# 16-bit pairs with power-of-two scales in the feed-forward products of a state-attention and hard-swish network

## The chip, the cores and the metric

The kernel runs on one core of a Trainium2 chip. The metric is the device time of one execution in microseconds; less is better. The engines are named as the profile names them: PE (TensorE, the matrix engine; PEld is its weight load), DVE (VectorE), ACT (ScalarE), POOL (GpSimd) and SP (SyncE, which here only issues transfers).

## The reference

Eight batches of `x` (8 heads, 512 tokens, 64 wide) are attended against 32 states per head, in both directions, and all 4352 result rows pass through a feed-forward network with 2048 hidden features:

```python
scores = scale * np.matmul(x, state.transpose(0, 1, 3, 2))
...
xread = np.matmul(a, state)                # 512 token rows of a batch
scores2 = scale * np.matmul(state, x.transpose(0, 1, 3, 2))
...
sread = np.matmul(a2, x)                   # 32 state rows of a batch
x = concatenate([xread, sread])            # rows of 512 = 8 heads x 64
h = x @ w_in                               # 512 x 2048
g = h * np.clip(h + 3.0, 0.0, 6.0) / 6.0
out = (g @ w_out).astype(np.float32)       # 2048 x 512
```

(The last lines are shortened; shapes are in the comments.) Everything is 32-bit at the inputs and at the output.

## The kernel before

**Products of pairs.** A number is kept as a pair: a rounded high part `hi` and the rest `lo`, both in the reduced 32-bit format `fp32r`. `split` (L329) makes a pair with two instructions, a copy on ACT that rounds and a subtraction on DVE. `product` (L1064) multiplies two pairs with three matmuls of 128x128 by 128x512: hi.hi, hi.lo and lo.hi.

**Steps.** The work is cut into steps n = 16b + i: batch b (0 to 7) and hidden block i (0 to 15, 128 features each). Step group b = 8 holds the state rows of all batches. In `first` (L1082) six matmuls make one block of h, transposed: the stationary operand is `wp` (the product of the batch's states with `w_in`, so that h comes straight from the attention weights), the moving one is `aT` (the attention weights). ACT and DVE then form `g` (L1127, L1129) and split it (L331, L332). In `second` (L1134), two steps later (`LAG`), twelve matmuls (4 blocks of 128 tokens, three each) add `g` times `w_out` into the banks acc0 to acc3; the stationary operand is `g`, the moving one is `w_out_hi` or `w_out_lo`. After block 15 ACT and DVE empty the four banks with the factor 1/6 (L1171, L1174). Matmuls of both kinds are recorded at L1071. For b = 8, `states_halves` splits curves that are already there, and `second` has two token blocks instead of four.

**Around the steps.** `attention` (L938) computes scores and softmax of a batch ahead of its steps. `wp` is made in `wprime` (L654, matmuls at L541) for b < 4; for b from 4 on eight products of `joined` (L585, matmuls at L608) make it for four batches together, write it to memory (`far_wp`), and `wprime_loaded` (L632) reads it back. `w_in_terms` (L1243) and `states_first` (L1263) do the first product of the state rows in a form with fewer multiplications.

**What sets the order.** All instructions are added to a `Plan` with an engine, a cost, a rank, and what they read and write. `Plan.order` (L121) first follows a list of numbers (`OPENING`) and then takes, engine by engine, what can start soonest, the smaller rank first. Pools have numbered slots, which the plan gives out. Each engine runs its list in order; the waits between engines follow from the data.

```python
for l, r in ((ah, bh), (ah, bl), (al, bh)):
    nc.tensor.matmul(ps, l, r, start=start and k == 0, stop=stop and k == n - 1)
```

Of the kernel before, what the change touches and what calls it, by code (L numbers as in the profile page):

```python
# [34 lines left out]

PLAIN = 1
STATES = [110, 111, 118, 0.5, 1.0]
EARLY = 5
BY_TWO = (0, 0)
TERMS = [76, 4, 3.0]  # L40
JOINED = 4
JOINED_AT = [33, 41, 42, 49, 57, 59, 60, 70]
# [3 lines left out]
LOADED = [-6, -6.5]  # L46
STAGED = [('wp', 'ot'), ('wp', 'ot'), ('ot', 'wp'), ('ot', 'aT'), ('ot', 'wp'), ('wp', 'aT'), ('aT', 'wp'), ('ot', 'ot')]
PREP = [4, -4]
SUMS = -3
CURVE = 2  # L50
# [34 lines left out]
class Plan:  # L85
# [14 lines left out]
    def add(self, engine, cost, rank, do, reads=(), writes=(), after=(), size=0):  # L100
        n = len(self.ops)
        deps = set(after)
# [13 lines left out]

    def slot_of(self, key):

        return key[:2] if key[0] in self.slots else None

    def order(self):  # L121
        opening = [int(n) for n in OPENING.split()]
# [20 lines left out]
        row, self.start, self.took = [], [0.0] * n_ops, [0.0] * n_ops  # L143
        while len(row) < n_ops:
            best = None
            told = opening[len(row)] if len(row) < len(opening) else None
            for e, numbers in open_ops.items():
                if told is not None:
                    numbers = {told} & numbers
                can = []  # L150
# [48 lines left out]
            open_ops[e].discard(n)  # L199
            for h in heirs[n]:  # L200
# [6 lines left out]
            row.append(n)  # L207
        return row
# [18 lines left out]
def tile_state_attention_then_hardswish_ffn(  # L227
# [90 lines left out]

    def get(key, make):

        if key[:2] not in made:
            made[key[:2]] = make()
        return made[key[:2]]
# [5 lines left out]
    def split(rank, hi, lo, src, reads, writes, cost=0.62):  # L329

        S_(cost, rank, lambda: nc.scalar.copy(hi(), src()), reads, [writes[0]])  # L331
# [32 lines left out]
    def weight(kind, k, n, place, rank, load_rank):  # L364
# [8 lines left out]
        def pieces():  # L373
            if place[0] == "raw":
                return get(place, lambda: stage.tile([P, 512, 2], U32, name="raw", **by_plan("raw", place))).unsqueeze(1)
            if place[0] == "ot":
                return get(place, lambda: outp.tile([P, 2, 512, 2], U32, name="wide", tag="ot"))
# [109 lines left out]
    def x_tile(b):  # L487
# [3 lines left out]
        t = get(x_key(b), lambda: att.tile([P, J, H, D], F32, name="xb", bufs=1))  # L491
# [24 lines left out]
    def load_turned(b, rank, after=()):  # L516


        for g in range(NG):
            key = ("raw", ("x", b, g))  # L520
            for i in range(2):
                for u in range(2):
                    for k in range(D // NS):
                        def load(g=g, i=i, u=u, k=k, key=key):
                            t = get(key, lambda: stage.tile([P, 2, S], F32, name="raw", **by_plan("raw", key)))
# [59 lines left out]
    def joined(p, m, s0):  # L585
# [25 lines left out]
        far = lambda: get(far_key, lambda: dram.tile([B - JOINED, 2, P, NG * CH], F32, name=f"far_wp{c}"))  # L611
        for i in reversed(range(NG)):
            key = (staged[i], ("joined", c, k, i))
            if staged[i] == "ot":
                both = lambda key=key: get(key, lambda: outp.tile([P, 2, NG, CH], F32R, name="wp", tag="ot"))
                of = lambda h, both=both: both()[:, ("hi", "lo").index(h)]
            else:
                pool = gp if staged[i] == "wp" else att
                of = lambda h, key=key, pool=pool: get((f"{key[0]}_{h}", key[1]), lambda: pool.tile(
                    [P, NG, CH], F32R, name=f"{key[0]}_{h}", **by_plan(f"{key[0]}_{h}", key)))  # L620
            tiles[i] = of
            for u in range(NG):
                split(URGENT, lambda of=of, u=u: of("hi")[:, u], lambda of=of, u=u: of("lo")[:, u],
                      lambda i=i, u=u: bank(ps[i, u]), [ps[i, u]], [(*key, u, "hi"), (*key, u, "lo")])
            for h in ("hi", "lo"):
                Q(rank, 524.0, lambda i=i, h=h, of=of: nc.sync.dma_start(
                    far()[:, ("hi", "lo").index(h), (NG * k + i) * NS : (NG * k + i + 1) * NS].rearrange("b n e -> n b e"), of(h).rearrange("p u f -> p (u f)").bitcast(F32)),
# [4 lines left out]
    def wprime_loaded(b, c, rank, after):  # L632

        far_key = ("far", ("wp", c))
        for h in ("hi", "lo"):
            Q(rank, 524.0, lambda h=h: nc.sync.dma_start(
                wp_of(b, c, h).rearrange("p u f -> p (u f)").bitcast(F32),
# [8 lines left out]
    def wp_of(b, c, half):  # L646
        key = wp_key(b, c)
        if key[0] == "ot":
            both = get(key, lambda: outp.tile([P, 2, NG, CH], F32R, name="wp", tag="ot"))
            return both[:, ("hi", "lo").index(half)]  # L650
        return get((f"wp_{half}", (b, c)), lambda: gp.tile(
            [P, NG, CH], F32R, name=f"wp_{half}", **by_plan(f"wp_{half}", ("wp", (b, c)))))

    def wprime(b, parts, rank, banks=None, after=()):  # L654
# [16 lines left out]
        for c, f0, _, n, fs, bs in work[::-1]:  # L671
            wp_at[b, c, f0] = at
            for u in range(NG):
# [4 lines left out]
                      [(*wp_key(b, c), f0, u, half) for half in ("hi", "lo")], cost)  # L678
# [97 lines left out]
    def weights_of(b):  # L776
        made["aT", b] = {h: (lambda h=h: get((f"aT_{h}", b),
                         lambda: att.tile(
            [P, NG, S], F32R, name=f"aT_{h}", **by_plan(f"aT_{h}", ("aT", b))))) for h in ("hi", "lo")}
        return made["aT", b]  # L780

    def tokens_by_rows(after, banks):
# [7 lines left out]
        whole = get(bt_key, lambda: outp.tile([P, J, DO], F32, name="ot")).rearrange(  # L790
# [82 lines left out]
    def tokens_by_columns(b, rank, ps):  # L873
# [8 lines left out]
        for g in range(NG):  # L882
# [90 lines left out]
    def weights_moved(b, rank, after=()):  # L973
# [18 lines left out]
        made_of = lambda key: get(key, lambda: stage.tile([P, NG, S], F32, name="raw", **by_plan("raw", key)))  # L992
# [83 lines left out]
    def first(n):  # L1076
# [37 lines left out]
        else:  # L1114
            first_of[n] = T(1.37, n, run, reads, [ps], [first_of[n - 1]] if n >= 34 else ())
# [6 lines left out]
        half = {h: (lambda h=h: get((f"g_{h}", n), lambda: gp.tile(  # L1122
            [P, S], F32R, name=f"g_{h}", bufs=3))[:, :width]) for h in ("hi", "lo")}
        cost = 0.1 + 0.53 * width / S

        rank = n if b < 1 else n - 1.5
        S_(cost + 0.05, rank, lambda: nc.scalar.activation(  # L1127
            g(), bank(ps)[:, :width], AF.Relu, bias=three), [ps], [g_key])
        V(cost, rank, lambda: nc.vector.scalar_tensor_tensor(  # L1129
            g(), g(), 6.0, bank(ps)[:, :width], op0=ALU.min, op1=ALU.mult), [ps], [g_key])  # L1130
        if not in_32:
            split(n, half["hi"], half["lo"], g, [g_key], [("g_hi", n), ("g_lo", n)], cost)

    part_of = {}  # L1134

    def second(n):
# [3 lines left out]
        for j in range(nt):  # L1140
# [3 lines left out]
            def run(js=js, acc=acc):  # L1144
# [4 lines left out]
                hi, lo = made["g_hi", n], made["g_lo", n]  # L1149
                w = [w_out_of(h, i, 1)[:, 0, :] for h in ("hi", "lo")]  # L1150
# [3 lines left out]
            else:  # L1154

                T(0.685, n + LAG + 0.5 + (1.2 if b == B and i == NF - 2 and j == nt - 1 else 0.0), run,
                  [("g_hi", n), ("g_lo", n), w_out_key(i, "hi"), w_out_key(i, "lo")], [acc])
# [4 lines left out]
        ot = lambda: get(ot_key, lambda: outp.tile([P, J, DO], F32, name="ot"))  # L1162
        for j in range(nt):
# [6 lines left out]
            elif (j % 2 == 0 or i < NF - 1) if b < B else j == nt - 1:  # L1170
                S_(0.62, rank, lambda j=j, acc=acc: nc.scalar.mul(ot()[:, j, :], bank(acc), 1.0 / 6.0),  # L1171
                   [acc], [(*ot_key, j)])
            else:
                V(0.68, rank, lambda j=j, acc=acc: nc.vector.tensor_scalar_mul(  # L1174
                    ot()[:, j, :], bank(acc), 1.0 / 6.0), [acc], [(*ot_key, j)])
# [18 lines left out]
    def sread_split(rank):  # L1194
# [7 lines left out]
            [*sread, ("aT", B, "hi")], [("aT", B, "lo")])  # L1202
        sums = ("raw", ("sums", B))
        part = lambda k: get(sums, lambda: stage.tile([P, NG, S], F32, name="raw", **by_plan("raw", sums))).rearrange(
# [15 lines left out]
        S_(1.2, rank, lambda: nc.scalar.copy(both["hi"](), whole()), parts, [("sums", B, "hi"), ("half", ("sums", B))])  # L1220
# [3 lines left out]

    pieces, operands, items, joined_of = [], [], [], {}
# [3 lines left out]

    def w_in_terms(p, m, rank, after):  # L1230

        w = lambda k, c: w_in_of(2 * p + c)[:, NG * k : NG * (k + 1), :]
# [332 lines left out]
```

## Time and profile before

| | |
|---|---|
| time of three runs, median (lowest to highest) | 638.12 us (637.46 to 638.59) |
| the profiled execution: its span, first to last instruction | 635.2 us; its own time is not listed apart, so the 2.9 us between span and median are taken as what lies around the span |
| busy time: PE, PEld, DVE, ACT, POOL | 629.2, 496.6, 431.0, 301.7, 3.1 us |
| mean granted TensorE clock | 0.998 of full speed (2.4 GHz) |

How to read it: a matmul is recorded from the entry of its first column to the end of its last result, so consecutive matmuls overlap in the record, and a busy PE says nothing of its rate. The rate is seen from start to start.

### The profile page before, as it was taken

How to read it: one execution, taken by the hardware profiler on the slowest of the kernel's cores; microseconds unless marked ns; L12 is line 12 of the kernel's file. 1: busy time of each engine (PE TensorE's matmuls, PEld its weight loads, DVE VectorE, ACT ScalarE, POOL GpSimd, SP SyncE). 2: the span in 40 equal slices, each digit the busy share in tenths (PEclk: the TensorE clock that was granted, in tenths of full speed). 3: DMA queues.
4: the chain of work that ended last, by engine and by line, in shares of the span. 5: the costliest groups of instructions: out<-in, count | busy, mean ns of one | idle time of the engine just before them, and what ended most of it. 6: DMA issues, size and time to landing. Idle time of an engine off the chain costs nothing.

```text
span 635.2 us, 9736 instructions
## 1 busy us (share of the span) xinstructions
PE 629.2 (99%) x3650; PEld 496.6 (78%) x3650; DVE 431.0 (68%) x719; ACT 301.7 (47%) x512; POOL 3.1 (0%) x11
## 2 busy tenths in 40 slices
PE   9999999999999999999999999999999999999997
PEld 7677687877777777778777887888878888888885
DVE  6898994678697557983578547974889464624632
ACT  6888664344445544553445534443544343333331
POOL 1000000000000000000000000000000000000000
PEclk9999999999999999999999999999999999999999
DMA  8987114455554677655795787635792569954031
GB/s 298 377 225 234 34 51 71 84 131 96 168 146 183 202 230 236 166 188 138 227 247 200 225 227 200 181 92 143 233 284 80 114 250 335 359 166 199 21 113 34
DMA packets 157007, 114.15 MB, mean 180 GB/s; under 512 B 128032, under 2 KB 136352, under 8 KB 155040
## 3 DMA queue, kind: packets, MB, share of 16 engines
q1 hardware_dynamic: 156816, 113.46, 59.2%
q8 instruction: 29, 0.48, 0.3%
q14 instruction: 18, 0.15, 0.1%
q10 hardware_dynamic: 144, 0.07, 0.0%
HBM read 66.83 MB, written 40.89 MB: 170 GB/s over the span
## 4 chain that ended last, share of the span: by engine, by line
PE 98%; DVE 1%; ACT 0%; issue 0%
PE acc L1071 59%; PE ps_h L1071 27%; PE ps_s L1071 3%; PE ps_s L541 3%; PE ps_h L1028 1%; PE ps_s L608 1%; PE ps_h L608 1%; PE ps_h L541 1%; PE acc L1146 1%; PE ps_h L1534 0%; PE acc L730 0%; PE ps_s L803 0%; PE ps_h L1106 0%; DVE w_in L412 0%; PE ps_s L1028 0%; PE ps_s L966 0%
## 5 line engine op out<-in xcount | busy, mean ns | idle before, releaser
L1071 PE MATMUL acc<-w_out_hi,g_hi 128*128 128x512 f32 x540 | 213.1, 395 | 0.0
L1071 PE MATMUL acc<-w_out_lo,g_hi 128*128 128x512 f32 x540 | 210.3, 389 | 0.0
L1071 PE MATMUL acc<-w_out_hi,g_lo 128*128 128x512 f32 x540 | 210.2, 389 | 0.0
L1127 ACT ACTIVATE g<-ps_h,three 128x512 f32<-128x512 f32 x128 | 88.0, 689 | 177.0 <-PE ps_h L1071 172.6
L1129 DVE SCALAR_TENSOR_TENSOR g<-g,ps_h 128x512 f32<-128x512 f32 x128 | 87.5, 685 | 96.4 <-ACT g L1127 95.3
L1071 PEld LDWEIGHTS acc<-w_out_hi,g_hi 128*128 128x128 f32 x540 | 101.3, 188 | 30.8 <-issue 9.1
L1071 PEld LDWEIGHTS acc<-w_out_hi,g_lo 128*128 128x128 f32 x540 | 101.4, 188 | 21.4
L1071 PEld LDWEIGHTS acc<-w_out_lo,g_hi 128*128 128x128 f32 x540 | 101.4, 188 | 20.2
L331 ACT CAST g_hi<-g 128x512 fp32r<-128x512 f32 x127 | 78.8, 621 | 72.7 <-DVE g L1129 53.1
L332 DVE TENSOR_TENSOR g_lo<-g,g_hi 128x512 fp32r<-128x512 f32 x127 | 86.9, 686 | 31.7 <-ACT g_hi L331 30.3
L1071 PE MATMUL ps_h<-aT_hi,wp_hi 128*128 128x512 f32 x182 | 72.0, 396 | 0.0
L1071 PE MATMUL ps_h<-aT_lo,wp_hi 128*128 128x512 f32 x182 | 70.8, 389 | 0.0
L1071 PE MATMUL ps_h<-aT_hi,wp_lo 128*128 128x512 f32 x182 | 70.8, 389 | 0.0
L1071 PE MATMUL ps_h<-aT_hi,wp 128*128 128x512 f32 x144 | 50.0, 389 | 0.0
L1071 PEld LDWEIGHTS ps_h<-aT_hi,wp_hi 128*128 128x128 f32 x182 | 34.2, 188 | 8.0 <-issue 0.7
L1071 PEld LDWEIGHTS ps_h<-aT_lo,wp_hi 128*128 128x128 f32 x182 | 34.2, 188 | 7.5 <-issue 0.5
L1071 PEld LDWEIGHTS ps_h<-aT_hi,wp_lo 128*128 128x128 f32 x182 | 34.2, 188 | 7.2
L1071 PEld LDWEIGHTS ps_h<-aT_hi,wp 128*128 128x128 f32 x144 | 27.0, 188 | 5.6
L1071 PE MATMUL ps_h<-aT_lo,wp 128*128 128x512 f32 x72 | 28.0, 389 | 0.0
L720 DVE STREAM_TRANSPOSE tmp<-raw 128x512 f32<-128x512 f32 x28 | 19.2, 698 | 1.9 <-DMA raw<-in_x_dram 1.9
L332 DVE TENSOR_TENSOR wp_lo<-ps_h,wp_hi 128x512 fp32r<-128x512 f32 x14 | 9.2, 686 | 10.3 <-ACT wp_hi L331 10.3
L332 DVE TENSOR_TENSOR g_lo<-w_in,g_hi 128x256 fp32r<-128x256 f32 x16 | 6.8, 426 | 13.7 <-ACT g_hi L331 13.6
(177 smaller groups left out, 583.6 us busy)
## 6 DMA issues: line engine op xcount, KB each, us to landing
terms<-far SPq DMA_DIRECT2D x14, 1024.0 KB, 7.8
xb<-in_x_dram SPq DMA_DIRECT2D x32, 256.0 KB, 4.3
out_dram<-ot SPq DMA_DIRECT2D x8, 1024.0 KB, 5.8
raw<-in_x_dram SPq DMA_DIRECT2D x112, 64.0 KB, 2.9
far<-half SPq DMA_DIRECT2D x14, 512.0 KB, 3.5
far<-raw SPq DMA_DIRECT2D x14, 512.0 KB, 4.0
far_wp<-wp SPq DMA_DIRECT2D x14, 512.0 KB, 4.1
wp_hi<-far_wp SPq DMA_DIRECT2D x11, 512.0 KB, 5.0
```

The lines of the kernel that those rows point to most:

```text
L331: S_(cost, rank, lambda: nc.scalar.copy(hi(), src()), reads, [writes[0]])
L332: V(cost, rank, lambda: nc.vector.tensor_tensor(lo(), src(), hi().bitcast(F32), op=ALU.subtract), [*reads, writes[0]], [writes[1]])
L541: nc.tensor.matmul(out[q // 2 if by_pairs else u][at * NS : (at + 1) * NS, :], made["stT", b][rows, cols], moving(q)[rows], start=True, st ...
L608: nc.tensor.matmul(bank(ps[i, u]), st(l)[rows, i], r()[rows, i], start=n == 0, stop=n == 2)
L720: V(0.7, rank[0], lambda q=q, key=key: nc.vector.transpose(xT(b, q), made[key][:, q % 2]), [(*key, q % 2, u, k) for u in range(2) for k in ...
L1028: nc.tensor.matmul(bank(pr)[cols, u * D : (u + 1) * D], e2T(b, u)[:, j * P + q * NS : j * P + (q + 1) * NS], x_tile(b)[:, NG * q + u, j, : ...
L1071: nc.tensor.matmul(ps, l, r, start=start and k == 0, stop=stop and k == n - 1)
L1127: S_(cost + 0.05, rank, lambda: nc.scalar.activation(g(), bank(ps)[:, :width], AF.Relu, bias=three), [ps], [g_key])
L1129: V(cost, rank, lambda: nc.vector.scalar_tensor_tensor(g(), g(), 6.0, bank(ps)[:, :width], op0=ALU.min, op1=ALU.mult), [ps], [g_key])
L1146: nc.tensor.matmul(bank(acc), made["g_hi", n][:, js], plain_out[i][1](), start=opens, stop=closes)
```

## The change

From the third batch on (b from 2, the code's `HALF_FROM`), the pairs of `wp`, `aT`, `g` and `w_out` are 16-bit floats (`F16`) instead of `fp32r`. A 16-bit float has a short exponent, so each operand is multiplied by a power of two first, and the powers come off again in the factors of L1226 (ACT's `scale`) and at the emptying of the banks. The powers are found on the chip: the largest absolute values of the states, of `w_in`, of `w_out` and of the state rows are reduced on DVE (`states_top`) or ACT (`w_out_tops`), sent to memory and back to all partitions (`scales_of`), and turned into exponents by bit operations. `converted` turns each of the 16 blocks of `w_out` into a 16-bit pair, once, with one ACT and two DVE instructions. The pairs sit in half of the bytes, in the tiles they had; the pairs of `w_out` need new homes, one slot of the pool `ot` and then tiles of `w_out` whose 32-bit pairs are no longer read. Other tiles so freed (`GROWN`) become further slots of `ot`, `xb` and `raw`. The transfers of `far_wp` move half the bytes. New instructions (`X`) are slipped into the list where it would wait; the list is cut at 851 rows, and several step numbers of the plan differ.

The diff, cut to its core:

```diff
+HALF_FROM = 2
+CONVERTED = [19, 20, 24, 26, 27, 27, 32, 26, 34, 40, 40, 41, 35, 42, 45, 46]
+GROWN = {3: "ot", 4: "xb", 5: "raw", 6: "raw", 7: "ot"}
...
-JOINED_AT = [33, 41, 42, 49, 57, 59, 60, 70]
+JOINED_AT = [33, 39, 48, 52, 58, 60, 62, 72]
...
+    def half_bits(t, n):
+        t = t.rearrange("p u f -> p (u f)") if len(t.shape) == 3 else t
+        return t.bitcast(F16)[:, :n]
+
+    def split(rank, hi, lo, src, reads, writes, cost=0.62, scale=None, add=None):
+
+        if scale is not None:
...
+            S(cost, rank, lambda: nc.scalar.mul(hi(), src(), by()), [*reads, *keys], [writes[0]])
+            V_(cost, rank, lambda: nc.vector.scalar_tensor_tensor(
+                lo(), src(), by(), hi() if hi().dtype == F16 else hi().bitcast(F32), op0=ALU.mult, op1=ALU.subtract),
+                [*reads, *keys, writes[0]], [writes[1]])
+            return
         S_(cost, rank, lambda: nc.scalar.copy(hi(), src()), reads, [writes[0]])
...
-        far = lambda: get(far_key, lambda: dram.tile([B - JOINED, 2, P, NG * CH], F32, name=f"far_wp{c}"))
+        far = lambda: get(far_key, lambda: dram.tile([B - JOINED, 2, P, NG * CH], F16, name=f"far_wp{c}"))
...
+        return half_bits(t, NG * CH).rearrange("p (u f) -> p u f", u=NG) if b >= HALF_FROM else t
...
-                      [(*wp_key(b, c), f0, u, half) for half in ("hi", "lo")], cost)
+                      [(*wp_key(b, c), f0, u, half) for half in ("hi", "lo")], cost, "sigma" if b >= HALF_FROM else None)
...
-                  [("aT", b, g, "hi"), ("aT", b, g, "lo")])
+                  [("aT", b, g, "hi"), ("aT", b, g, "lo")], 0.62, A_SCALE if b >= HALF_FROM else None)
...
+        scaled = b >= HALF_FROM
+        forms[n] = scaled and i in in_16
...
         S_(cost + 0.05, rank, lambda: nc.scalar.activation(
-            g(), bank(ps)[:, :width], AF.Relu, bias=three), [ps], [g_key])
+            g(), bank(ps)[:, :width], AF.Relu, bias=three, scale=scales["1/h"]() if scaled else 1.0),
+            [ps, *([("scale", "1/h")] if scaled else [])], [g_key])
...
-                hi, lo = made["g_hi", n], made["g_lo", n]
-                w = [w_out_of(h, i, 1)[:, 0, :] for h in ("hi", "lo")]
+                hi, lo = (g_halves(n)[h]() for h in ("hi", "lo"))
+                w = [] if forms[n] else [w_out_of(h, i, 1)[:, 0, :] for h in ("hi", "lo")]
+                if forms[n]:
+                    w = [w_16_of(i)[:, e] for e in range(2)]
                 product(bank(acc), [((hi[:, js], lo[:, js]), w)], opens, closes)
...
-                S_(0.62, rank, lambda j=j, acc=acc: nc.scalar.mul(ot()[:, j, :], bank(acc), 1.0 / 6.0),
-                   [acc], [(*ot_key, j)])
+                S_(0.62, rank, lambda j=j, acc=acc: nc.scalar.mul(ot()[:, j, :], bank(acc), ends()),
+                   [acc, *end_keys], [(*ot_key, j)])
...
+    def states_top(name, k, src, reads, cost, rank, after=()):
+        X("V", cost, rank, lambda: nc.vector.tensor_reduce(
+            found(name, k), src(), axis=AX.X, op=ALU.max, apply_absolute_value=True),
+          reads, [("top_of", name, k)], after)
...
+        X("Q", 0.55, rank, lambda: nc.sync.dma_start(far().rearrange("(p k) -> p k", k=n), here()),
+          [("here", names, i) for i in range(n)], [("far", ("top", names))], (), 20.0)
+        X("Q", 0.55, rank, lambda: nc.sync.dma_start(tmp(all_key)[:, : P * n], far().partition_broadcast(P)),
+          [("far", ("top", names))], [all_key], (), 120.0)
+        X("V", 0.5, rank, lambda: nc.vector.tensor_reduce(
+            here(), tmp(all_key)[:, : P * n].rearrange("p (q k) -> p k q", k=n), axis=AX.X, op=ALU.max),
+          [all_key], [("here", names, i) for i in range(n)])
...
+            X("S", 0.85, rank, lambda k=k, junk=junk: nc.scalar.activation(
+                tmp(junk), w_out_of("hi", k, 1)[:, 0].bitcast(F32), AF.Abs,
+                accum_out=found("w_out", k)), [w_out_key(k, "hi")], [junk, ("top_of", "w_out", k)], after)
...
+        X("S", 0.62, rank, lambda: nc.scalar.mul(w_16_of(k)[:, 0], w("hi"), alpha()), [hi_key, *key], [hi16], after)
+        X("V", 0.7, rank, lambda: nc.vector.scalar_tensor_tensor(
+            w_16_of(k)[:, 1], w("hi"), alpha(), w_16_of(k)[:, 0], op0=ALU.mult, op1=ALU.subtract),
+            [hi_key, hi16, *key], [lo16], after)
+        X("V", 0.7, rank, lambda: nc.vector.scalar_tensor_tensor(
+            w_16_of(k)[:, 1], w("lo"), alpha(), w_16_of(k)[:, 1], op0=ALU.mult, op1=ALU.add),
+            [lo_key, *key], [lo16], after)
```

**What moves, on PE.** PE's list is the same row for row up to the first block of h of the third batch (b = 2, i = 0), two steps before its first `second`. There it reads before (`ps_h` is the bank, `aT` the moving, `wp` the stationary operand):

```order
L1071 MATMUL acc2_1191<-w_out_hi3_910,g_lo_1634 128x512
L1071 MATMUL ps_h_1728<-aT_hi_1691,wp_1648 128x512
L1071 MATMUL ps_h_1728<-aT_lo_1703,wp_1648 128x512
L1071 MATMUL ps_h_1728<-aT_hi_1691,wp_1648 128x512 x2
...
L1071 MATMUL acc0_1202<-w_out_hi3_910,g_hi_1656 128x512
```

and in the change:

```order
L1166 MATMUL acc2_1235<-w_out_hi3_933,g_lo_1738 128x512
L1166 LDWEIGHTS wp_1755
L1166 MATMUL ps_h_1842<-aT_hi_1802,wp_1755 128x512
L1166 LDWEIGHTS wp_1755
L1166 MATMUL ps_h_1842<-aT_lo_1814,wp_1755 128x512
...
L1166 MATMUL acc0_1248<-w_out_hi3_933,g_hi_1764 128x512
```

A 32-bit matmul is one instruction that loads its weights itself; a 16-bit one is two, the load and the matmul. 1824 matmuls take the second form: 576 of `first`, 1248 of `second` (96 of them for the state rows). The number of matmuls is the same.

**What moves, on DVE.** This is DVE's list around steps 21 to 23, before:

```order
L332 TENSOR_TENSOR g_lo_1218<-g_1188,g_hi_1211 128x512
L1129 SCALAR_TENSOR_TENSOR g_1224<-g_1224,ps_h_1151 128x512
L332 TENSOR_TENSOR g_lo_1241<-g_1148,g_hi_1235 128x512
L332 TENSOR_TENSOR wp_lo_1287<-ps_h_1255,wp_hi_1270 128x512
L332 TENSOR_TENSOR g_lo_1295<-g_1224,g_hi_1289 128x512
...
L332 TENSOR_TENSOR wp_lo_1304<-ps_s_1245,wp_hi_1276 128x512
L332 TENSOR_TENSOR g_lo_1341<-g_1309,g_hi_1338 128x512
L1129 SCALAR_TENSOR_TENSOR g_1360<-g_1360,ps_h_1347 128x512
```

and in the change (`top_` and `here_` are maxima, `tmp` holds what came back from memory, `sc_` the powers of two, `w16` a 16-bit pair of `w_out`):

```order
L422 TENSOR_TENSOR g_lo_1293<-g_1186,g_hi_1286 128x512
L1359 TENSOR_REDUCE here_w_out_1341<-top_w_out_627 128x1
...
L1347 TENSOR_REDUCE top_w_in_504<-w_in3_698 128x1 x4
...
L1359 TENSOR_REDUCE here_state_643<-top_w_in2_1348 128x1
...
L422 TENSOR_TENSOR wp_lo_1374<-ps_s_1297,wp_hi_1330 128x512
L1366 TENSOR_REDUCE here_w_out_1341<-tmp_1393 128x1
L422 TENSOR_TENSOR g_lo_1416<-g_1379,g_hi_1412 128x512
...
L1366 TENSOR_REDUCE here_state_643<-tmp_1395 128x2
...
L1226 SCALAR_TENSOR_TENSOR g_1440<-g_1440,ps_h_1404 128x512
L1436 SCALAR_TENSOR_TENSOR w16_1471<-w_out_hi0_337,sc_w_out_1442,w16_1471 128x512
L1439 SCALAR_TENSOR_TENSOR w16_1471<-w_out_lo0_353,sc_w_out_1442,w16_1471 128x512
```

At steps 19 to 23 come in 13 of the 16 maxima of `w_in`, two reductions that wait for data from memory, and 17 other small instructions on the maxima and powers; the 32 conversions come between the instructions of steps 25 to 47. The products of `joined` move too: on PE's list they stood ahead of the first products of steps 40, 43, 45, 48, 56, 64, 70 and 72, and now of 44, 48, 51, 53, 56, 58, 64 and 70.

## Rows read from the trace of the kernel before

**Rows 1.** The page: busy time by engine, granted clock, chain that ended last.
```profile
span 635.2 us, 9736 instructions
PE 629.2 (99%) x3650; PEld 496.6 (78%) x3650; DVE 431.0 (68%) x719; ACT 301.7 (47%) x512; POOL 3.1 (0%) x11
PEclk9999999999999999999999999999999999999999
PE 98%; DVE 1%; ACT 0%; issue 0%
```

**Rows 2.** All waits of PE: who, for whom, us in total, times, longest.
```profile
engine line waited for: us in total, times, longest us
PE ps_h L1534 <- PEq L1549: 0.8, 1, 0.8
PE acc L1146 <- DVE g L1129: 0.2, 1, 0.2
PE acc L842 <- DVE w_in L831: 0.2, 1, 0.2
```

**Rows 3.** The chain in order of time: start us, us, what, matmuls.
```profile
157.01 5.44 PE acc L1071 x24
600.68 29.93 PE acc L1071 x132
```

**Rows 4.** PE's bf16 matmuls near the start: start us, us to the last end, count.
```profile
4.71 0.38 PE L1534 MATMUL ps_h<-const-bfloat16-1.0 128*128 128x256 bf16 x2
11.52 0.28 PE L1534 MATMUL ps_h<-const-bfloat16-1.0 128*128 128x256 bf16 x1
12.44 1.06 PE L1534 MATMUL ps_h<-const-bfloat16-1.0 128*128 128x256 bf16 x8
12.33 0.88 PEld L1534 LDWEIGHTS <-const-bfloat16-1.0 128*128 128x128 bf16 x8
```

**Rows 5.** Instructions by line and shape: busy us, mean ns of one, idle before.
```profile
L1071 PEld LDWEIGHTS acc<-w_out_lo,g_hi 128*128 128x128 f32 x540 | 101.4, 188 | 20.2
L1129 DVE SCALAR_TENSOR_TENSOR g<-g,ps_h 128x512 f32<-128x512 f32 x128 | 87.5, 685 | 96.4 <-ACT g L1127 95.3
L755 DVE TENSOR_REDUCE m<-tmp 128x16 f32<-128x512 f32 x14 | 9.5, 677 | 0.0
L928 DVE TENSOR_SCALAR nm<-nm 128x1 f32<-128x1 f32 x14 | 2.0, 150 | 0.3
L1252 DVE TENSOR_TENSOR raw<-w_in,half 128x1024 fp32r<-128x1024 f32 x8 | 9.6, 1201 | 0.1
L1127 ACT ACTIVATE g<-ps_h,three 128x512 f32<-128x512 f32 x128 | 88.0, 689 | 177.0 <-PE ps_h L1071 172.6 <-DVE g_lo L332 1.6 <-ACT half L1251 1.4
L1171 ACT ACTIVATE ot<-acc 128x512 f32<-128x512 f32 x17 | 10.0, 597 | 5.6 <-PE acc L1071 5.5
L331 ACT CAST g_hi<-g 128x512 fp32r<-128x512 f32 x127 | 78.8, 621 | 72.7 <-DVE g L1129 53.1 <-PE acc L1071 19.3
L407 ACT CAST tops<-early 128x512 f16<-128x512 bf16 x17 | 12.8, 779 | 4.5 <-DMA early<-in_moe_w_out_dram 3.1 <-DMA early<-in_moe_w_in_dram 1.4
```

**Rows 6.** Stretches: us, busy time (instructions) of each engine, clock, DMA share, GB/s.
```profile
56.00:76.00 20.00, 20.00 (x170) 14.81 (x169) 18.91 (x33) 14.23 (x26) 0.00 (x0) 1.00 0.25 67
83.00:216.00 133.00, 133.00 (x806) 103.51 (x805) 94.94 (x166) 63.58 (x109) 0.00 (x0) 1.00 0.48 118
```

**Rows 7.** DMA issues: KB each, median us from issue to landing.
```profile
raw<-in_x_dram SPq DMA_DIRECT2D x112, 64.0 KB, 2.9
wp_hi<-far_wp SPq DMA_DIRECT2D x11, 512.0 KB, 5.0
w_in<-C SPq DMA_DIRECT2D x32, 64.0 KB, 2.0
```

**Rows 8.** ACT empties the first bank of the first and the third batch.
```profile
94.76 0.60 ACT L1171 ACTIVATE ot<-acc 128x512 f32<-128x512 f32 x1 [0.44 <-PE acc L1071]
243.65 0.60 ACT L1171 ACTIVATE ot<-acc 128x512 f32<-128x512 f32 x1
```

More of the change, by code (lines that the diff above doesn't have):

```diff
@@ L98, in __init__, with add @@
         self.ops, self.writer, self.readers, self.users = [], {}, {}, {}
-    def add(self, engine, cost, rank, do, reads=(), writes=(), after=(), size=0):
+        self.told, self.extra = [], set()
+        self.grown, self.growing = {}, []
+    def add(self, engine, cost, rank, do, reads=(), writes=(), after=(), size=0, extra=False):
         n = len(self.ops)
+        if not extra:
+            self.told.append(n)
+        else:
+            self.extra.add(n)
         deps = set(after)
@@ L143, in order @@
         row, self.start, self.took = [], [0.0] * n_ops, [0.0] * n_ops
+        placed = set()
         while len(row) < n_ops:
             best = None
-            told = opening[len(row)] if len(row) < len(opening) else None
+            while opening and opening[0] in placed:
+                opening.pop(0)
+            told = opening[0] if opening and not waits[opening[0]] else None
+            if told is not None:
+                e = self.ops[told][0]
+                t = max(clock[e], ready[told])
+                for x in sorted(self.extra & open_ops[e], key=lambda x: (self.ops[x][2], x)) if len(row) > EXTRA_FROM else ():
+                    at = max(clock[e], ready[x])
+                    room = all(slot in held or any(f[0] <= at for f in free[slot[0]]) for slot in self.ops[x][5])
+                    if room and at + self.ops[x][1] <= t + (1.0 if e == "Q" else SQUEEZE):
+                        told = x
+                        break
+            more = opening and told is None and any(self.extra & s for s in open_ops.values())
             for e, numbers in open_ops.items():
@@ L1131, in first, with g_halves, whole @@
         if not in_32:
-            split(n, half["hi"], half["lo"], g, [g_key], [("g_hi", n), ("g_lo", n)], cost)
-    part_of = {}
+            split(n, half["hi"], half["lo"], g, [g_key], [("g_hi", n), ("g_lo", n)], cost,
+                  (G_SCALE if forms[n] else "g_wide") if scaled else None)
+    part_of, forms = {}, {}
+    def g_halves(n):
+        def whole(h):
+            t = get((f"g_{h}", n), lambda: gp.tile([P, S], F32R, name=f"g_{h}", bufs=3))
+            return half_bits(t, S) if forms[n] else t
+        return {h: (lambda h=h: whole(h)) for h in ("hi", "lo")}
     def second(n):
@@ new lines, in tile_state_attention_then_hardswish_ffn, with region, w_16_of @@
+    w_16 = {}
+    def region(n, shape, dtype, name):
+        c, half = REGIONS[n]
+        return cpool.tile(list(shape), dtype, name=name, tag=f"w_out_{half}{c}")
+    def w_16_of(k):
+        c = k // FPC
+        if c not in w_16:
+            shape = (P, FPC, 2, DO)
+            w_16[c] = (get(("ot", ("w16", 0)), lambda: ot_tile(("ot", ("w16", 0)), shape, F16, "w16")) if c == 0
+                       else region(c - 1, shape, F16, "w16"))
+        return w_16[c][:, k % FPC]
+    region_free = {}
```

252 lines of the change are left out of this document (199 added, 53 removed).

## The prediction, made before the changed kernel was run

> **What bounds the kernel now.** I read the page first. PE is busy 629.2 of 635.2 us and makes 98% of the chain that ended last, at the full granted clock in every slice; DVE has 68%, ACT 47% [rows 1]. Next the waits: all that PE ever waited for another engine is 1.2 us, and none of the three rows lies in the steps (L1534 is the filler at the start, L1146 and L842 belong to the first block) [rows 2]. So no wait can be removed. What is left is the pace of the matmuls themselves, which a busy share hides, because records overlap. The chain in order of time shows it: the last 132 matmuls take 29.93 us, 226.7 ns each, and a stretch of 24 in the middle of the kernel takes 5.44 us, 226.7 again [rows 3]. The pace is the same everywhere, so it is a property of the instruction. 512 columns at 2.4 GHz stream in 213.3 ns; 13.4 ns of each matmul are something else. The weight load of an `fp32r` matmul takes 188 ns beside the matmul before it [rows 5].
>
> **The pace of the 16-bit matmuls, the main term.** 1824 matmuls (576 of `first`, 1248 of `second`) become 16-bit. The trace has no 16-bit matmul of 512 columns, but bf16 ones of 256, the filler. Eight of them lie 1.06 us from first start to last end, one alone takes 0.28: (1.06 - 0.28) / 7 = 111.4 ns from start to start, 4.7 over the 106.7 that 256 columns need; two others are some 0.10 apart (0.38 - 0.28) [rows 4]. They have the same two instructions, load and matmul, as the changed kernel's list, and the loads run beside the matmuls: eight loads lie within 0.88 us, 0.11 each [rows 4]. The bounds: nothing over the streaming, 213.3; 4.7 ns for each matmul, 218.0; 4.7 ns for each 256 columns, 222.8; no change, 226.7. I take 216.0, between the first two: in the filler the loads are as close-packed as the matmuls, so part of the 4.7 may be theirs, and with 512 columns they have twice the room. That is 226.7 - 216.0 = 10.7 ns, times 1824: **-19.5 us** (ends: -24.4 at 213.3, -15.9 at 218.0, -7.1 at 222.8, 0 at 226.7).
>
> The 1824 added loads I cost at nothing: each hides under the matmul before it, as in the filler. Without that cover each would cost its 0.11 us, 201 us in all. A rule of the Trainium skill says so: "TensorE: Matmul & The Clock Gate", Part 3, "The mechanism", has a weight load overlap running matmuls only where the row groups differ, and here all pairs fill all rows. By it the pair would take 216 + 110 = 326 ns and the kernel 821 us. The filler fills all 128 rows too and is spaced 0.11, not 0.22 [rows 4]; the trace disagrees with the rule.
>
> **DVE.** It gets 13 maxima of `w_in` at 0.677, 32 conversions at 0.685 (the `SCALAR_TENSOR_TENSOR` of L1129) and 19 small ones at 0.15 [rows 5]: 8.8 + 21.9 + 2.9 = 33.6 us in steps 19 to 47. In the trace of before these steps lie roughly from 83 to 216 us, between shortly before the first batch's banks are emptied (94.76) and some steps before the third's (243.65) [rows 8]. There DVE is busy 94.9 of 133 us [rows 6]. Two of the three products of `joined` that stood there move out, each with four evictions and a residual, 4 x 0.685 + 1.20 = 3.9 us [rows 5]: -7.9. Need: 120.6 us. The stretch shrinks by 15 steps x 18 x 10.7 ns = 2.9, to about 130: DVE would be 93% busy. From 56 to 76 us it was 18.91 of 20 busy, 95%, and PE lost nothing [rows 6, 2], since a block of `g` has two steps (8 us) between its first matmuls and its use. So I put 1.5 us of waits on PE for the whole change, near the lower end (below zero is excluded, as PE has no waits to give back; the upper end is the rival below).
>
> **The waits for memory.** The maxima travel to memory and back, two transfers of 2.0 to 5.0 us, if small ones land like the nearest rows [rows 7]: 4 to 10 us. Between the sending of the states' maxima and the reduction that waits for them DVE has seven 0.685 instructions and six small ones, 5.7 us; it may stand for up to 4 us. Behind it in its queue are two blocks of `g`, whose users come two steps later; 4 us fit into 8. On SP, which waits for the maxima before it can send them, the loads of the third batch's `x` stand behind; DVE's transposes want them at step 25, PE's products at step 35, ten steps of 4.1 us later. Cost: 0.
>
> **ACT.** 32 instructions of at most 0.78 us (the row that writes 16 bits) [rows 5] are 25 us, in a stretch where it is busy 63.6 of 133 [rows 6]. A factor read from memory makes instructions longer: L1127, which reads its bias so, takes 689 ns, L1171, which reads none, 597 [rows 5]; so 0.09 us more on each. ACT stays under 60%, and the chain of a block of `g` goes from 2.68 to about 2.8 us of 8. Only in the last emptying does the 0.09 lie on the path: +0.1. The halved transfers of `far_wp` and the new slots speed up nothing that anything waited for; cost and gain 0.
>
> **Sum.** 635.2 - 19.5 + 1.5 + 0.1 = 617.3 us of span, with the 2.9 around it **620.2 us**, 2.8% below the median of 638.12.
>
> **Rivals.**
> 1. *DVE becomes the bound, slower than before.* No row shows a `SCALAR_TENSOR_TENSOR` with a factor read from memory and a 16-bit result. 57 of them lie in the stretch (32 conversions, 25 splits from step 32 on). The room is 130 - 120.6 = 9.4 us. At 0.85 us each (1.25 times, as ACT's row with 16-bit results has against the one without) the room is just used up. To eat the 18 us of gain as well they must take 0.685 + 27.4 / 57 = 1.17 us. At double price (1.37) PE would wait 39 - 9.4 = 30 us: 649 us. For it: nothing; against: 0.685 for the same operation. 3%.
> 2. *The same, in part, or a conversion or slot that comes too late.* The last conversions stand two or three steps ahead of their use. 5 to 15 us of waits: 625 to 634. 9%.
> 3. *The change brings no faster pace.* If the 13.4 ns come from a new stationary operand in every matmul and not from the format, the pace stays 226.7: 639.7 us. The bf16 filler, with a load in every matmul too, speaks against it. 3%. If the excess grows with the columns (222.8): 632.6. 4%.
> 4. *Loads in series*, as above: pace 326, 821 us, under 1%. The other way out is a pace below the streaming time: 131 ns would give -95.7 x 1824 = -175 us, 465 us. The same page of the Trainium skill ("Back-to-back issue gap") has 131 ns as what a stream of loads and matmuls of 512 columns sustains. Rows 3 show 226.7 for that and the filler over 100 for half the columns, so it is not this chip's pace here: under 1%.
>
> **How the numbers follow.** My forecast, 213.3 to 218.0 ns and waits of 0 to 5 us, holds 80%. Its best corner is 615.3, its worst 628. The range 616 to 628 leaves out 3 in 100 below and some 16 above (most of rival 2, and rivals 1, 3 and 4). Less than 0.2% either way (636.8 to 639.4) is about what a measurement of this kernel cannot tell from no change. Faster: forecast, rival 2, the slower pace of rival 3, 131 ns: 0.93. Same: half of the unchanged pace, 0.02. Slower: rival 1, the other half, serial loads: 0.05.
>
> **What would show it.** Right: chains of `second` in the last steps at 216 ns per matmul (132 in 28.5 us), the first 32 steps unchanged at 226.7; loads of some 0.1 us that overlap; PE's waits a few us, on DVE or ACT, around steps 40 to 47 if anywhere; DVE over 90% in 83 to 216 us; the added `SCALAR_TENSOR_TENSOR` at 0.69. Wrong: a pace over 220; PE waiting for `g_lo` or `w16` for 5 us or more in all; a mean granted clock below 0.99.

## The result, and the profile after

The changed kernel takes 631.8 us (median of 4 runs, 630.27 to 633.1), the kernel before 638.01 on the same chip (median of 4): a ratio of 0.9901, 95% interval 0.9883 to 0.9918. It is faster by 1.0%, where 2.8% and 620.2 us had been forecast; the time lies outside the range of 616 to 628. The profiled execution has a span of 628.5 us and took 630.27.

The page of the changed kernel, lines that answer to [rows 1], and the granted clock in 40 slices:
```profile
span 628.5 us, 9864 instructions
PE 614.4 (98%) x3650; PEld 332.9 (53%) x3650; DVE 470.2 (75%) x799; ACT 336.9 (54%) x560; POOL 3.1 (0%) x11
PEclk9999999979999999999999999999999999999999
PE 89%; SPq 3%; DMA 3%; DVE 3%; issue 1%; ACT 1%; DVEq 0%; ACTq 0%
```
PE has given up 14.8 us of busy time; DVE has gained 39.2 and ACT 35.2. Two things are new: a dip of the clock in the ninth slice (126 to 141 us), and a chain of which PE has 89% and no longer 98%. 9 points of it are SP's queue, DMA and DVE.

All waits of PE of 0.3 us and more, against [rows 2], and under them the one long wait of DVE for a transfer:
```profile
engine line waited for: us in total, times, longest us
PE ps_h L1166 <- DVE g L1226: 6.3, 1, 6.3
PE ps_h L698 <- DVE g L1226: 0.8, 1, 0.8
PE ps_h L1797 <- PEq L1812: 0.8, 1, 0.8
PE ps_h L1166 <- DMA wp_hi<-far_wp: 0.6, 1, 0.6
PE ps_s L1166 <- ACT g L1223: 0.3, 1, 0.3
...
DVE here_w_out L1366 <- DMA tmp<-far_w_out: 8.1, 1, 8.1
```
A single wait makes the difference. The chain in order of time shows what made it (start us, us, what):
```profile
101.32 6.99 PE acc L1166 x30
...
113.91 7.61 DMA far_w_out<-here_w_out
121.59 0.34 SPq L1364
...
129.22 0.69 DVE g L1226
...
129.96 2.93 PE ps_h L1166 x6
...
595.34 28.50 PE acc L1166 x132
```
The maxima of `w_out`, 0.5 KB, are sent to memory at 113.91 and land 7.61 us later. Only then may SP issue the read-back, and DVE, which has come to the reduction that wants it, stands. The maxima were there earlier: DVE has them at 108.17, but SP has other transfers ahead of the store in its list and issues it 5.7 us later:
```profile
108.00 0.17 DVE L1359 TENSOR_REDUCE here_w_out<-top_w_out 128x1 f32<-128x16 f32 x1
113.91 0.52 SPq L1362 DMA_DIRECT2D far_w_out<-here_w_out  x1
```
The DMA issues between 105 and 130 us (KB each, median us from issue to landing) give both ways:
```profile
tmp<-far_state SPq DMA_DIRECT2D x1, 128.0 KB, 4.7
tmp<-far_w_out SPq DMA_DIRECT2D x1, 64.0 KB, 4.5
far_w_out<-here_w_out SPq DMA_DIRECT2D x1, 0.5 KB, 7.6
```
So the way through memory took 7.6 + 4.5 us, and 18 us from the maxima to the reduction. Had the store gone out at once and all else stayed, the data would have been there at some 120.4, and DVE, free at 117.98, would have stood for 2.4 us and not 8.1 (an estimate from these rows; no run shows it). DVE resumes at 126.11, works off one residual and the small instructions of both scales, and writes the awaited `g` at 129.22; PE has then been idle for 6.3 us. Stretches (busy us of PE, PEld, DVE, ACT, POOL, then clock, DMA share, GB/s):
```profile
120.00:125.00 5.00, 3.63 (x16) 2.62 (x14) 0.00 (x0) 0.69 (x1) 0.00 (x0) 1.00 0.07 18
125.00:130.00 5.00, 0.04 (x1) 0.04 (x1) 3.58 (x18) 2.02 (x3) 0.00 (x0) 0.76 0.88 168
130.00:134.00 4.00, 4.00 (x10) 3.17 (x11) 3.96 (x7) 1.53 (x3) 0.00 (x0) 0.50 0.01 3
140.00:160.00 20.00, 20.00 (x110) 14.93 (x111) 18.39 (x34) 11.40 (x21) 0.00 (x0) 1.00 0.53 123
160.00:180.00 20.00, 20.00 (x100) 13.63 (x99) 18.70 (x34) 12.34 (x20) 0.00 (x0) 1.00 0.45 79
```
After the idle time the clock is at 0.50, which is 1.2 GHz of the two levels: ten matmuls start between 129.96 and 134.39 us, 443 ns each where 227 is usual, which costs 10 x 0.216 = 2.2 us more. From 140 us on DVE is busy for 92 to 94% and PE waits for nothing.

The two paces stand in the chain above. 132 matmuls at the end take 28.50 us and not 29.93 [rows 3], 215.9 ns each: the 16-bit ones. But 30 `fp32r` matmuls of `second`, which the change doesn't touch, take 6.99 us, 233.0 ns each. In the kernel before the same 30 stand so in the chain:
```profile
100.11 6.80 PE acc L1071 x30
```
That is 226.7 ns. By the means of the starts in the trace, 350 such matmuls take 233.1 ns each and not 227.1, 177 of `first` 229.9 and not 226.9, and 71 that read `terms` 232.3 and not 226.7: together about 3.0 us more.

Four terms make the account of the span: 635.2 - 19.7 (1824 x 10.8 ns) + 8.0 (waits of 9.2 us and not 1.2) + 2.2 (clock) + 3.0 (`fp32r`) = 628.7, against 628.5 measured.

### The profile page after: what moved, and what is told of

Same layout as the page of the kernel before. It is cut to its first block, busy times and chain, and to the rows that moved or that the text cites. A ratio compares the mean times of both kernels' runs of the same rounds, so it can differ in the third digit from the quotient of the medians.

```text
span 628.5 us, 9864 instructions
## 1 busy us (share of the span) xinstructions
PE 614.4 (98%) x3650; PEld 332.9 (53%) x3650; DVE 470.2 (75%) x799; ACT 336.9 (54%) x560; POOL 3.1 (0%) x11
## 4 chain that ended last, share of the span: by engine, by line
PE 89%; SPq 3%; DMA 3%; DVE 3%; issue 1%; ACT 1%; DVEq 0%; ACTq 0%
PE acc L1166 52%; PE ps_h L1166 25%; PE ps_s L1166 3%; PE ps_s L631 3%; SPq L617 2%; DMA raw<-in_x_dram 1%; DMA far_w_out<-here_w_out 1%; PE ps_h L1123 1%; SPq L1097 1%; PE ps_s L698 1%; PE ps_h L631 1%; PE ps_h L698 1%; PE acc L1250 1%; DMA wp_hi<-far_wp 1%; PE ps_h L1797 1%
## 5 line engine op out<-in xcount | busy, mean ns | idle before, releaser
L1166 PE MATMUL acc<-w,g_hi 128*128 128x512 f16 x832 | 247.7, 379 | 0.0
L1166 PE MATMUL acc<-w,g_lo 128*128 128x512 f16 x416 | 157.7, 379 | 0.0
L1223 ACT ACTIVATE g<-ps_h,three,sc_state 128x512 f32<-128x512 f32 x96 | 74.6, 777 | 124.2 <-PE ps_h L1166 122.0
L1226 DVE SCALAR_TENSOR_TENSOR g<-g,ps_h 128x512 f32<-128x512 f32 x128 | 87.2, 683 | 65.1 <-ACT g L1223 64.5
L1166 PEld LDWEIGHTS <-g_hi 128*128 128x128 f16 x832 | 79.2, 98 | 100.3 <-issue 8.1
L1166 PE MATMUL acc<-w_out_hi,g_hi 128*128 128x512 f32 x124 | 50.6, 408 | 0.0
L1166 PE MATMUL acc<-w_out_hi,g_lo 128*128 128x512 f32 x124 | 49.2, 397 | 0.0
L1166 PE MATMUL acc<-w_out_lo,g_hi 128*128 128x512 f32 x124 | 49.2, 396 | 0.0
L1223 ACT ACTIVATE g<-ps_h,three 128x512 f32<-128x512 f32 x32 | 21.9, 688 | 25.5 <-PE ps_h L1166 19.7
L1166 PEld LDWEIGHTS acc<-w_out_hi,g_hi 128*128 128x128 f32 x124 | 23.6, 190 | 10.0 <-issue 3.3
L1166 PEld LDWEIGHTS acc<-w_out_hi,g_lo 128*128 128x128 f32 x124 | 23.4, 189 | 5.8
L1166 PEld LDWEIGHTS acc<-w_out_lo,g_hi 128*128 128x128 f32 x124 | 23.6, 190 | 5.3
```

Source lines behind the costliest of these rows:

```text
L1223: S_(cost + 0.05, rank, lambda: nc.scalar.activation(g(), bank(ps)[:, :width], AF.Relu, bias=three, scale=scales["1/h"]() if scaled else 1.0),
L1226: V(cost, rank, lambda: nc.vector.scalar_tensor_tensor(g(), g(), 6.0, bank(ps)[:, :width], op0=ALU.min, op1=ALU.mult), [ps], [g_key])
```

## The experiments

Two theories were tried in the first four runs, W for the wait and P for the pace.

**The read held back.** VectorE's order alone is changed:
```
+READ_AT = 28
-        X("V", 0.5, rank, lambda: nc.vector.tensor_reduce(
+        late_read = X("V", 0.5, rank, lambda: nc.vector.tensor_reduce(
...
+        if names[0] != "sread":
+            at(READ_AT + 1, lambda: plan.ops[late_read][4].add(first_of[READ_AT]))
```


> The changed kernel with one edit: VectorE's two reductions that read the gathered maxima back are held until the first matmul of block 28 is issued; the transfers stay as they are. Theory W (the loss is the stand of 8.1 us of VectorE for the maxima's way through memory, which made TensorE wait 6.3 us at 124 us and cost about 2.3 us more at the clock 0.50 to 0.76 behind it): that wait and the low clock go, 631.8 - 8.5 = 623.3 us, TensorE's waits for g fall from 6.3 us to under 1 us. Rival F (VectorE is too full there: what is not lost at the read is lost behind it, since the weight conversions now come later): the waits move to 135 to 165 us and the time stays within 629 to 633 us.

Measured: 636.13 us, ratio 0.9983 (0.9966 to 1.0001), slower than the changed kernel. The theory in this form fell, and so did the numbers of the rival. The wait at 124 us was gone, but PE was busy for only 14.91 of 20 us from 160 to 180 us, and SP still stood 4.8 us for the store, with loads of `x` behind it that DVE now waited 7.6 us for. The edit did more than take the wait away: the first reduction ran at 148.34 us and not at 126.11, so the scales were known 22 us later, and the conversions crowded behind them. The run therefore doesn't say what an earlier scale would give.

**Another queue.** Both transfers on GpSimd's queue:
```
-        X("Q", 0.55, rank, lambda: nc.sync.dma_start(far()...
+        X("P", 0.55, rank, lambda: nc.gpsimd.dma_start(far()...
-        X("Q", 0.55, rank, lambda: nc.sync.dma_start(tmp(all_key)...
+        X("P", 0.55, rank, lambda: nc.gpsimd.dma_start(tmp(all_key)...
```


> The changed kernel with one edit: the maxima's transfers (store and read back) are issued by GpSimd's queue and not by SyncE's, behind whose loads of x they stood. Theory W: store and read-back land in some 2 to 3 us each, not 7.6 and 4.5 us, VectorE waits under 1 us for them, and the time is 622 to 625 us, as with the read held back. Rival F: 629 to 633 us. Rival M (the way through memory itself is that long on any queue): the store takes 6 us or more here too.

Measured: 633.78 us, 0.9931 (0.9908 to 0.9954). Rival M is right for the landing: the store left at 108.81 here, with no queue ahead of it, and took longer still, so its 7.6 us are not SP's queue. DMA issues from 105 to 140 us of this run:
```profile
tmp<-far_w_out POOLq DMA_DIRECT2D x1, 64.0 KB, 3.6
far_w_out<-here_w_out POOLq DMA_DIRECT2D x1, 0.5 KB, 8.9
```
The read-back was issued at 131.20 only, and the trace has GpSimd waiting for a PE product ahead of it:
```profile
POOL tmp L1364 <- PE ps_s L631: 18.5, 1, 18.5
```
The stretches:
```profile
120.00:125.00 5.00, 5.00 (x24) 4.03 (x23) 1.58 (x3) 1.89 (x3) 0.00 (x0) 1.00 0.65 110
140.00:160.00 20.00, 16.48 (x87) 11.65 (x87) 16.20 (x38) 10.65 (x19) 0.00 (x0) 0.91 0.47 82
160.00:180.00 20.00, 16.70 (x79) 11.29 (x85) 19.02 (x35) 12.40 (x20) 0.00 (x0) 0.98 0.51 138
```
The planner set the reduction 39 of DVE's instructions later here, at 148.86 us, so nothing stood at 124 us. DVE was busy 1.58 of 5 us all the same, and PE missed 6.8 us between 140 and 180 us. As in the run before, the scales came some 22 us later than in the changed kernel, so neither run shows what a shorter way through memory would give; the first was slower than the changed kernel, and this one no faster.

**Small tiles wider, by 160 bytes in all** (`N_MAX = 20` to `28`):

> The changed kernel with the five small tiles of maxima 28 wide and not 20, nothing else: every tile behind them begins 32 bytes beyond a multiple of 64 again, as in the kernel before. Theory P (the fp32r products of the second half of the feed-forward went from 226.7 to 233.2 ns because the small tiles moved g and the others onto multiples of 64): 226.7 ns again, some 540 matmuls x 6.5 ns = 3.5 us less, 628.3 us. Rival R (the pace of fp32r is a matter of the run or the chip, or of another of the kernel's differences): 233 ns as before and 631.8 us.

Measured: 631.54 us, 0.9900 (0.9878 to 0.9922); the `fp32r` matmuls of `second` took 231 ns in the mean up to 165 us. P in this form, the remainder by 64, fell.

**32 unused bytes in the kernel before**, a `cpool.tile([P, 1], F32, name="pad")` made after all other tiles of the pool:

> The kernel before with one unused tile of 32 bytes behind the others of its pool, so that the operands (aT, wp, g) begin at multiples of 64 bytes as in the changed kernel; w_out stays. Theory P: its 1572 fp32r products of the second half at 233 ns and not 227: 638.0 + 1572 x 6.3 ns = 647.9 us. Rival R: 638 us, and the pace 227 ns.

Measured: 650.45 us, 1.0196 (1.018 to 1.0211), and the chain has the 30 matmuls with 7.00 us:
```profile
102.39 7.00 PE acc L1071 x30
```
One unused tile makes the kernel before 12.7 us slower. So addresses do set the pace, but not by the remainder by 64 alone.

The second four runs took up the two lessons: make the scales known sooner, and put the operands where they were.

**The maxima spread on the chip.**
```
-        X("Q", 0.55, rank, lambda: nc.sync.dma_start(far()...
-        X("Q", 0.55, rank, lambda: nc.sync.dma_start(tmp(all_key)...
+        for i in range(n):
+            X("V", 0.2, rank, lambda i=i: nc.vector.tensor_scalar_mul(
+                wide()[:, i], ident, here()[:, i : i + 1]), ...
+        for i in range(n):
+            X("T", 0.25, rank, lambda i=i: nc.tensor.matmul(
+                bank(ps)[:, i * P : (i + 1) * P], nc.const_aps.tensor(1.0, [P, P], F32),
+                wide()[:, i], start=True, stop=True), ...
```
with the reduction reading `bank(ps)` instead of `tmp`.

> The changed kernel with the maxima's way through memory (store, read back to all partitions) replaced by a way on the chip: VectorE makes a diagonal of each column of maxima (128x128), one fp32 product with ones spreads it over the partitions into a PSUM bank, and the same reduction reads the bank. VectorE's order is otherwise almost the same, unlike in the two runs before, whose conversions came some 30 instructions later. Theory W2 (what costs is that the scales are known 8 us late while VectorE has nothing to do that does not need them, and from then on it is too full to catch up, so that holding the read back only moved the wait to 160 to 180 us): VectorE stands under 1.5 us here, TensorE's wait of 6.3 us at 124 us and the low clock behind it go, no other wait of over 2 us comes, 631.8 - 8.5 = 623.3 us, 622 to 625. Rival F (VectorE is too full whatever the scales' time): waits of 4 us and more at 130 to 180 us, 628 to 632 us.

Measured: 623.57 us, 0.9781 (0.9764 to 0.9798). W2 said 623.3. DVE stands 1.3 us for the product with ones, PE's longest wait for another engine is 0.9 us, the clock stays at 1.00, and the stretches that lost time above lose none:
```profile
DVE here_w_out L1371 <- PE ps_s L1368: 1.3, 1, 1.3
```
```profile
120.00:125.00 5.00, 5.00 (x23) 4.08 (x22) 2.80 (x10) 2.25 (x4) 0.00 (x0) 1.00 0.46 90
140.00:160.00 20.00, 20.00 (x111) 14.38 (x110) 18.31 (x31) 14.87 (x25) 0.00 (x0) 1.00 0.42 73
160.00:180.00 20.00, 20.00 (x162) 12.00 (x160) 18.19 (x34) 11.01 (x18) 0.00 (x0) 1.00 0.56 107
```
DVE is as full as before and PE waits for none of it in these stretches. So a full DVE is not what cost (rival F); 8 us in which it could do nothing did. The edit takes two things away at once, the transfers and the 5.7 us that the store stood in SP's list; the run doesn't part them.

**Small tiles in the last pool.** `cpool.tile` becomes `small.tile(..., bufs=1)` for the maxima and scales, nothing else.

> The changed kernel with its small tiles (maxima, scales) in the last pool, behind all others, so that every operand of TensorE stands at the very address that it had in the kernel before. Theory P (addresses set the pace of the fp32r products; not the multiple of 64 alone, since 32 bytes more did nothing in the changed kernel): fp32r products of the second half at 226.7 ns and not 233, 348 of them and some 200 others x 6.3 ns = 3.5 us less, 628.3 us. Rival R (another difference of the two kernels slows them, such as VectorE's and ScalarE's added reads): 233 ns and 631.8 us.

Measured: 631.79 us, 0.9913 (0.9893 to 0.9933). The pace went as P said: the `fp32r` matmuls of `second` are at 227.6 ns in the mean up to 165 us, not 233.1. The time did not follow. The chain ahead of the store runs here through SP's queue, which issues one load after the other until 114.65 us, and then through the store (8.12 us) and the read-back (4.01); the store does not start sooner because PE is faster.
PE's wait there grew from 6.3 to 7.1 us, the low clock lasted longer (0.71 from 134 to 138 us, 0.95 in the changed kernel), and waits for `wp` and `terms` from memory took 1.9 us:
```profile
PE ps_h L1166 <- DVE g L1226: 7.6, 2, 7.1
PE ps_h L1166 <- DMA wp_hi<-far_wp: 1.2, 1, 1.2
PE ps_s L1166 <- DMA terms<-far: 0.7, 1, 0.7
```

**Both edits:**

> Both edits together: maxima spread by a product with ones, small tiles in the last pool. W2 and P: 631.8 - 8.5 - 3.5 = 619.8 us, 618.5 to 621.5, below both kernels. W2 alone: 623. P alone: 628.

Measured: 622.48 us, 0.9777 (0.9753 to 0.9802), 1.1 us less than with the first alone, where P had said 3.5 and the paces measured with the moved tiles give some 2.3. The two intervals overlap, so the 1.1 us are not clear of noise. 1.8 + 0.8 us of waits for `wp_hi` and `wp_lo` near 310 us have come in, whose loads stand in SP's queue behind 16 loads of `x`.

**64 unused bytes in the kernel before**, at the same place as the 32:

> The kernel before with 64 unused bytes behind its first pool and not 32. Theory P64 (only the remainder by 64 counts): 226.7 ns in the second half's products and 638 us. Rival PR (the distance to w_out counts in a finer or larger step): 229 to 233.5 ns and 642 to 650 us.

Measured: 650.06 us (one run), the 30 matmuls at 7.00 us. P64 fell, PR is right.

The last four runs were to settle what about the addresses counts, and to see whether the rest can be had.

**Both edits, and the loads of `wp` a block sooner** (`LOADED = [-8, 4.0]` to `[-9, 4.0]`):

> Both edits of the run of 622.5 us (maxima spread by a product with ones, small tiles in the last pool) and a third: the operands read back from memory may be issued one block earlier (-9 and not -8), so that SyncE's queue has them ahead of 16 loads of x. In that run TensorE waited 1.8 + 0.8 us for them near 310 us. If this wait was all that ate the gain of the addresses: 622.5 - 2.6 = 619.9 us. If another transfer is late in its place: 621 to 624 us.

Measured: 621.03 us, 0.9727 (0.9714 to 0.974), the fastest of all: 1.1 us above the first forecast, though no transfer was late in its place. No wait for `wp` is left; PE's longest wait for another engine is 0.9 us:
```profile
PE ps_h L1166 <- DVE g L1226: 0.9, 1, 0.9
PE ps_h L698 <- DVE g L1226: 0.7, 1, 0.7
PE ps_s L1166 <- DMA terms<-far: 0.4, 1, 0.4
```

**All tiles moved by 64 bytes together** (`pad = cpool.tile([P, 16], F32)` ahead of `tops`):

> The kernel before with 64 unused bytes ahead of all its large tiles: all of them move by 64, and no distance between two operands changes. Theory D (the distance from the moving operand w_out to g, or of two tiles in general, sets the pace of the fp32r products): 226.7 ns and 638 us. Rival A (the address itself counts): 233 ns and 650 us.

**Only the pools with the stationary operands moved by 64** (`att.tile([P, 16], F32, bufs=1)` at the end of its pool):

> The kernel before with 64 unused bytes between two pools, so that only wp, g, g_hi and g_lo (stationary operands, and what VectorE and ScalarE write there) move, against w_out, aT and the rest, which stay. Theory D, if it is moving against stationary operand: the second half's products at 233 ns and the first half's (aT against wp) slower too, 650 us and more. If only the distance between g and w_out counts: as with 64 bytes behind the first pool, 650 us, the first half's at 227 ns. Rival A with the address of aT or of the other tiles as the cause: 638 us.

**1024 unused bytes** in place of the 32 and 64:

> The kernel before with 1024 unused bytes behind its first pool. If the distance counts by its remainder at some power of two up to 1024: 226.7 ns and 638 us. If it does not repeat by then, or is no remainder: 229 to 233.5 ns and 643 to 650 us.

Measured, one run each: 637.36, 652.36 and 638.66 us. The 30 matmuls in the three chains, in this order:
```profile
100.51 6.80 PE acc L1072 x30
```
```profile
102.73 7.00 PE acc L1071 x30
```
```profile
100.91 6.80 PE acc L1071 x30
```
A common move costs nothing, so it is the distance (theory D), and the distance between moving and stationary tiles: in the second run `aT` and `w_out` stay where they were. There the six matmuls of a block of `first`, `aT` against `wp`, are slower too:
```profile
418.75 1.40 PE ps_h L1071 x6
```
against this in the kernel before:
```profile
417.20 1.36 PE ps_h L1071 x6
```
In this run two thirds of the `wp` tiles stand in the pool that moved and one third in one that didn't: by the means of the starts the six matmuls take 233.1 to 233.5 ns each with the first, and 230.7 with the second. Not all of it follows from a matmul's own two tiles, though. With 64 bytes behind the first pool `aT` and `wp` keep their distance, and a block of `first` is slower all the same:
```profile
302.30 1.38 PE ps_h L1071 x6
```
Its second matmul takes 233.4 ns in the mean, its sixth 228.0, so a part may carry over from the slowed matmuls ahead of it; that is not shown. The slow pace doesn't follow the other engines' load: the last 117 matmuls of that run keep 233.3 ns each, with DVE busy for 27 to 42% of the time and the DMA engines at 0.01 from 627 to 640 us:
```profile
612.91 27.30 PE acc L1071 x117
```
1024 bytes more make no difference; 32, 64, and the 736 and 896 of the changed kernel and of the one with wider small tiles all do. What lies behind it stays open: other distances were not tried, nor which distances would be faster still than those of the kernel before. The 16-bit matmuls show none of it: the last 132 take 28.50 us at the old distances as at the new ones.

## Why the prediction was wrong, point by point

- **The main term was right.** 16-bit matmuls at 216.0 ns: 215.9 measured, so -19.7 us and not -19.5. The trace agrees that the added loads cost nothing. They take 98 ns and lie under the matmul before:
```profile
L1166 PEld LDWEIGHTS <-g_hi 128*128 128x128 f16 x832 | 79.2, 98 | 100.3 <-issue 8.1
L417 DVE SCALAR_TENSOR_TENSOR g_lo<-g,g_hi 128x512 f16<-128x512 f32 x96 | 65.7, 687 | 23.5 <-ACT g_hi L416 21.9
L1223 ACT ACTIVATE g<-ps_h,three,sc_state 128x512 f32<-128x512 f32 x96 | 74.6, 777 | 124.2 <-PE ps_h L1166 122.0
```
  Both rivals from the Trainium skill ("TensorE: Matmul & The Clock Gate", serial loads and 131 ns) fell with this row and the chain.
- **DVE and ACT were nearly right.** The split with a factor from memory and a 16-bit result takes 687 ns, so rival 1 (1.17 us) fell; the 32 conversions, put at 685, take 741 and 743 ns, 1.8 us in all. ACT's pointer factor adds 89 ns (777 against 688 for the same line without it). The sign "DVE over 90% in 83 to 216 us" was missed in the changed kernel, 112.7 of 133 us or 85%, since DVE stood; in the best kernel it holds, 121.8 us or 92%. That costs little: the best kernel's waits come to 3.6 us against 1.2, where 1.5 more had been put.
- **"The waits for memory ... Cost: 0" failed.** This is the step that made the prediction wrong. Four numbers in it were off, and all in one direction. The store was taken to leave as soon as the maxima are there, with SP waiting for them; they waited for SP, 5.7 us for those of `w_out`, the ones that DVE then stood for. Secondly, the transfers were priced from medians over the whole kernel [rows 7], 4 to 10 us for both; they took 12.1. A median of landing times says little of one store: a third one, 1 KB at 510.91 us, landed after 3.2 us, with the DMA engines at 0.08 and less, where the one at 113.91 had them at 0.68 (114 to 116 us). That the other loads make the difference is likely and not shown. (The Trainium skill, "DMA: Bandwidth & Descriptors", "Anatomy of one DMA — SWDGE (gpsimd) path", has a fit of 2 us and the bytes at 436 GB/s for GpSimd's path; an estimate by it is 2.0 us for 0.5 KB and 2.2 for 64. On that path the run shows 8.9 and 3.6, on SyncE's 7.6 and 4.5.) Thirdly, DVE "may stand for up to 4 us" became 8.1. And fourthly, 4 us were weighed against 8 us of slack for `g` without the 3.1 us (126.11 to 129.22) of residual and small scale work that stands behind the wait and ahead of `g`. The run with the product in place of the transfers gave 8.2 us back (7.7 by the ratios to the kernel before), so this term, with the clock behind it, is shown; how it divides between SP's list and the transfers is not.
- **The clock.** That an idle PE comes back at half speed was in no term. It follows from the wait: 2.2 us on top of 6.3, and none where the wait is gone.
- **"The first 32 steps unchanged at 226.7" failed**, a sentence that stood only among the signs to look for. The `fp32r` matmuls went to 233.0, since 736 bytes of small tiles changed the distance between their operands: 3.0 us with the other `fp32r` products. So "a property of the instruction" was wrong as well, for this format. The trace of before could not show it; no row there has a second distance.
- **The rivals.** Rival 2, waits of 5 to 15 us and 625 to 634 us, is what came, at 9%. It named a conversion or slot that comes too late; it was the scale that they all need.
- **The sum** was near what the change can give: 621.0 us with three edits, against 620.2. Taken at the profiled run, 620.0 us of span against 617.3, 0.9 of the 2.7 us are waits beyond those forecast and 1.6 the busy time of the added products; the rest was not followed up. What lies around the span is 1.8 us in these runs, where 2.9 had been put, so the closeness of 621.0 and 620.2 is in part luck. The "best corner" of 615.3 leaves out the waits of 0 us: by the prediction's own terms it is 613.8, and the worst 627.3. The result doesn't hang on it.

## What to carry to other kernels

A value that later work on a nearly full engine waits for should not go through memory: price the round trip from the queue's state at that moment, with what stands ahead of the store in it, and count everything behind the wait. Moving the read 22 us back in the order helped neither run that did it. A maximum over partitions can be spread by a diagonal and one product with ones: here the reduction that wants it ran 7.5 us after the maxima were there and not 18, and DVE stood for 1.3 us and not 8.1. And whenever a change adds a small tile, compare the pace of matmuls that it doesn't touch: in a kernel bound by TensorE new tiles belong behind the operands, not between them.

## What the runs showed of the hardware

- The distance in SBUF between a matmul's moving and stationary tiles sets the pace of 512-column `fp32r` matmuls: 226.7 or 233 ns, and some 230 for matmuls behind slowed ones. 32 unused bytes cost 12.7 us in 638, 1024 nothing, and 64 ahead of everything nothing. The Trainium skill ("SBUF — State Buffer", "Who interferes with whom") has contention only on the port that VectorE and GpSimd share; these runs show a slower TensorE with GpSimd idle, and don't show why.
- A 0.5 KB store to memory landed after 7.6 us on SyncE's queue and 8.9 on GpSimd's, while transfers of small packets were under way (13467 of 13724 packets from 105 to 130 us under 512 B); one of 1 KB at 510.91 us, with nearly none, after 3.2.
- After 6.3 us without work TensorE ran ten matmuls at 0.50 of its clock before it was back at 1.00.
